# Attention and a Mish layer on one core: where a unit's first attention output is made

## The chip, the cores and the metric

The kernel runs on one core of one Trainium2 chip. The metric is the device time of one execution in microseconds, the median of several runs. Engines are called as the profile calls them: PE (matrix products), PEld (its weight loads), DVE (vector), ACT (activation), POOL and SP (which issues DMAs here).

## The reference

The inputs are q, k and v of 8 batches, 12 heads, 448 positions and 64 columns. For each head

```
scores = (q @ k.T) / 8
m      = max(scores, axis=-1)
e      = exp(scores - m)
attn   = e / (sum(e) + exp(-m) + 1e-9)
x      = attn @ v
```

The heads are put side by side into a matrix x of 3584 x 768. Then h = x @ w_in (768 x 2048), g = h * tanh(log(1 + exp(h))), which is the Mish function, and the result is g @ w_out (2048 x 768), in float32.

## The kernel before

**Pairs, units and stages.** Two heads make a pair; there are 48 pairs, six to a batch. From pair 6 on the kernel works in units of three pairs (`UNIT_PAIRS`), half a batch. The loop over `u` issues them: `p0 = 3 * u`, and unit `u` has two stages. In the first, 12 steps (`for n in range(steps)`) work on the scores of the unit's own pairs, on the attention outputs of the unit before, and on the last matrix product of earlier batches. In the second (`for f in range(FF_U)`) `mm1_mish` makes eight blocks of h and puts them through Mish; between them stand the denominators, the normalising of the unit's exponentials, their transposes by DMA, and the first scores of the next unit.

**A score group.** `scores(idx)` makes one of four groups of a pair. A group takes a score tile (`sc_tiles`, three tiles of two banks each). From pair 12 on (`DIAG_FROM`) the first three groups of a pair have two matmuls, one to each bank, and the fourth (`s == STEPS - 1`) has one, so its second bank is free. DVE then takes the maximum over the tile (L346). `exps(idx)` has ACT make the exponentials from the tile (L359), which gives the tile back. `scores_ahead` keeps three groups in the air: at step n of a unit group n + 3 is made, counted from 0 within the unit, while the exponentials are those of group n. Groups 0 to 2 of the next unit are made in the second stage.

**An attention output.** `av_pair(p)` (L459) multiplies the transposed exponentials `eT` of a pair by `v`: 8 matmuls in four pairs of 64 columns (L476). It goes into the bank that is given to it, or takes one with `mo_take`. The copy of the result to `xT` by DVE (a cast, L489) is put on the list `late`, and is issued at the next `flush_late()`, which stands at the start of every step behind the exponentials (L688), and wherever a part of the output product begins. `av_with` holds which output goes with which pair: `scores` makes it in front of the pair's fourth group, in the free second bank of that group's tile. So the three outputs of the unit before are made at steps 0, 4 and 8, each ahead of groups 3, 7 and 11.

**The output product.** `mm2_part(g, i, q0, nq)` makes a part of 128 rows and 192 or 384 columns (`nq` 1 or 2) in one bank: 16 matmuls (L565), issued two at a time as chunks. There are two such banks, `mo_tiles`, in the queue `mo_free`, which the second stage uses too. A part takes its bank with its first chunk. When its last chunk is issued, its copy to `o_sb` by DVE (L548) goes on `late`, and with that copy the bank goes back to the end of `mo_free`. An engine works through what is issued to it in order, so the place of that copy in DVE's row is where the list is flushed.

**The order of the chunks.** `plan` gives the parts of a unit. For odd `u` from 5 on their widths are 1, 2, 2, 2, for even `u` from 6 on 2, 2, 2, 1; the sum over the chunks is 56 in both. `weight` says how much is to be done by which step: 5.2 at step 0, 1.0 at each of steps 1 to 8, 0.4 at steps 9 to 11, of 14.4. That makes 20, 24, 28, 32 by the end of steps 0 to 3 in even units. A part of width 2 counts 16. So there the first part ends at step 0, the second at step 3, and the third begins at step 4. In odd units the parts end at 8, 24 and 40, the second at step 1, and the third begins at step 2. Within a step the order is: exponentials, flush, chunks, scores (with the output ahead of them).

**Other buffers that an output touches.** `eT` has three buffers, written by DMA transposes that SP issues in the second stage; `v_bf` has eight, written by POOL at step 0 of a unit; `xT` has two, one for each batch in work, and `mm1_mish` reads it.

Of the kernel before, what the change touches and what calls it, by code (L numbers as in the profile page):

```python
# [15 lines left out]
UNIT_PAIRS = 3  # L16
# [3 lines left out]
def kernel(  # L20
# [90 lines left out]
    av_with, av_read, rb = {}, {}, {}  # L111
# [6 lines left out]
    def mo_take():  # L118

        if not mo_free:  # L120
            flush_late()
        return mo_free.popleft()
# [104 lines left out]
    def apart(later, *earlier):  # L227

        for e in earlier:
            tc.declare_no_dep(later.ins, e.ins, reason="they read different PSUM banks")  # L230
# [63 lines left out]
    def free_half(p):  # L294

        return sc_tiles[(p * STEPS + STEPS - 1) % len(sc_tiles)][:, 1, :]

    def scores_ahead(limit):

        while rg["next"] < limit and rg["used"] < len(sc_tiles):  # L300
            rg["used"] += 1
            scores(rg["next"])
            rg["next"] += 1

    def scores(idx):

        p, s = divmod(idx, STEPS)
        if s == 0:
            if p < HP or p % UNIT_PAIRS == 0:
                for nm in ("negm", "sums", "expm", "den", "rden"):  # L310
                    stats[nm] = st_pool.tile([128, UNIT_PAIRS, NTILE], FP32, tag=nm, name=nm)
            at = 0 if p < HP else p % UNIT_PAIRS
            att[p] = {nm: t[:, at, :] for nm, t in stats.items()}
            att[p].update(en=en_bufs[p % N_EN], whole=dict(stats))
        st = att[p]
        qT, kT = qkT[p]
        kA, kB = kT[0:64, :], kT[64:128, :]
        sc = sc_tiles[idx % len(sc_tiles)]
        if s == STEPS - 1 and p in av_with:
            av_pair(av_with.pop(p), bank=sc[:, 1, :], beside=idx)  # L320
        if p >= DIAG_FROM:
            cols = tuple(range(2 * s, min(2 * s + 2, NTILE)))
            negm = st["negm"][:, cols[0] : cols[-1] + 1]
            for bk, i in enumerate(cols):
                nc.tensor.matmul(  # L325
                    sc[:, bk, 0:S], lhsT=qT[:, i].rearrange("d h r -> d (h r)"), rhs=kT,
                    start=True, stop=True,
                )
        elif s < 3:
            qa, qb = 128 * s, 64 + 128 * s  # L330
            nc.tensor.matmul(
                sc[:, 0, 0:S], lhsT=qT[0:64, qa : qa + 128], rhs=kA, start=True, stop=True
            )
            nc.tensor.matmul(
                sc[:, 1, 0:S], lhsT=qT[64:128, qb : qb + 128], rhs=kB, start=True, stop=True
            )
            cols, negm = (s, 4 + s), st["negm"][:, s : s + 5 : 4]
        else:
            nc.tensor.matmul(
                sc[0:64, 0, 0:S], lhsT=qT[0:64, 384:S], rhs=kA, start=True, stop=True  # L340
            )
            nc.tensor.matmul(
                sc[64:128, 0, 0:S], lhsT=qT[64:128, 0:64], rhs=kB, start=True, stop=True
            )
            cols, negm = (3,), st["negm"][:, 3:4]
        half_max[p] = nc.vector.tensor_reduce(  # L346
            out=negm, in_=sc[:, 0 : len(cols), 0:S], axis=AX.X, op=ALU.max, negate=True
        )
        st["sc", s] = (sc, cols)
# [109 lines left out]
    def av_pair(p, bank=None, beside=None, half=None, hold=False):  # L459
        b, hp = p // HP, p % HP  # L460
        eT = att[p]["eT"]
        v_bf = casted[p]["v"]
        if b not in xT:
            xT[b] = xT_pool.tile([128, DM_T, S], BF16, tag="xT", name="xT")
        if half is not None:
            bank = free_half(half)
            mms = av_beside.setdefault(half * STEPS + STEPS - 1, [])
        av = mo_take() if bank is None else bank
        for j in range(NT):
            for h in range(2):  # L470
                if p >= DIAG_FROM:
                    by_h = eT[0:SP_, j, :].rearrange("c (i h r) -> c h i r", h=2, r=64)
                    e_h = by_h[:, h]
                else:
                    e_h = eT[0:SP_, j, h * S : (h + 1) * S]
                mm = nc.tensor.matmul(  # L476
                    av[h * 64 : (h + 1) * 64, 0:S],
                    lhsT=v_bf[:, h, j * D : (j + 1) * D],
                    rhs=e_h,
                    start=(j == 0), stop=(j == NT - 1),  # L480
                )
                if half is not None:
                    apart(mm, half_max[half])
                    mms.append(mm)

        def evac():
            to = xT[b][:, hp, :]
            if p >= LATE_DIV:
                read = nc.vector.tensor_copy(out=to, in_=av[:, 0:S])  # L489
            else:  # L490
                read = nc.vector.tensor_tensor(
                    out=to, in0=av[:, 0:S], in1=rb.pop(p), op=ALU.mult
                )
            if half in half_exp:
                apart(read, half_exp[half])
            elif beside is not None or half is not None:
                av_read[beside if half is None else half * STEPS + STEPS - 1] = read
            if bank is None:
                mo_free.append(av)

        if p in spread_copy:
            late.append(spread_copy.pop(p))
        (held if hold else late).append(evac)
        del att[p], casted[p], qkT[p]
# [73 lines left out]
    first_mm2 = 2 * UNITS_PER_B  # L578
# [89 lines left out]
    for u in range(UNITS_PER_B, N_UNITS + 2 * UNITS_PER_B):  # L668
# [4 lines left out]
        total, done, acc = sum(w for _, w in filler), 0, 0.0  # L673
        p0 = u * UNIT_PAIRS
        if attn and u >= first_mm2:
            av_with.update({p0 + i: p0 + i - UNIT_PAIRS for i in range(UNIT_PAIRS)})
        nxt = p0 + UNIT_PAIRS
        end = min(nxt, N_PAIRS) * STEPS

        for n in range(steps):  # L680
            pi, s = divmod(n, STEPS)
            p, idx = p0 + pi, p0 * STEPS + n
# [22 lines left out]
            if n in LOAD_AT and u <= first_mm2 + 1:  # L705
                at = p0 + LOAD_AT.index(n)
# [41 lines left out]
            if u - UNITS_PER_B < len(W_AT):  # L748
                at = (u - UNITS_PER_B, n)
# [6 lines left out]
        for f in range(FF_U):  # L756
# [19 lines left out]
            if f in (3, FF_U - 1) and p0 >= LATE_DIV:  # L776
                p = todo[1 + f // (FF_U - 1)]
# [33 lines left out]
```

## Time and profile before

| what | value |
|---|---|
| median of 3 runs | 474.99 us |
| lowest and highest | 473.56 and 478.71 us |
| the profiled execution | 473.76 us |
| its span, first to last instruction | 472.0 us |
| mean granted clock of PE | 0.989 |
| PE busy | 449.1 us (95%) |
| DVE busy | 365.2 us (77%) |
| ACT busy | 332.4 us (70%) |
| matmuls of attention outputs (L476) into score banks | 336 recorded, 39.8 us |
| matmuls of the output product (L565) | 1024, 166.7 us |

How to read the views: a row of a timeline has the start in us from the span's start, the length in us, the engine, the line of the kernel, the operation, what it writes and reads with sizes, and the number of like instructions that were put together in the row. In brackets stands how long the engine was idle ahead of it, and what ended that. Rows of one engine can overlap a little, since instructions are pipelined. In the chain of waits a row has a start, a length and what the time went to.

### The profile page before, as it was taken

How to read it: one execution, taken by the hardware profiler on the slowest of the kernel's cores; microseconds unless marked ns; L12 is line 12 of the kernel's file. 1: busy time of each engine (PE TensorE's matmuls, PEld its weight loads, DVE VectorE, ACT ScalarE, POOL GpSimd, SP SyncE). 2: the span in 40 equal slices, each digit the busy share in tenths (PEclk: the TensorE clock that was granted, in tenths of full speed). 3: DMA queues.
4: the chain of work that ended last, by engine and by line, in shares of the span. 5: the costliest groups of instructions: out<-in, count | busy, mean ns of one | idle time of the engine just before them, and what ended most of it. 6: DMA issues, size and time to landing. Idle time of an engine off the chain costs nothing.

```text
span 472.0 us, 8866 instructions
## 1 busy us (share of the span) xinstructions
PE 449.1 (95%) x3051; PEld 246.8 (52%) x3051; DVE 365.2 (77%) x715; ACT 332.4 (70%) x877; POOL 103.0 (22%) x186
## 2 busy tenths in 40 slices
PE   6888999999998999999999999999999999999996
PEld 3344555545554555555555555555555555556563
DVE  5988848669897999999999999999899989421021
ACT  5999878888784869788796868687877869211300
POOL 4623555115023040311313040404040100000000
PEclk8889999999999999999999999999999999999999
DMA  8999999999899999999999999999999594921122
GB/s 228 239 205 230 235 219 212 176 255 202 199 272 244 233 251 223 264 238 227 272 251 241 228 252 209 292 201 254 235 291 226 159 214 121 231 71 33 35 65 69
DMA packets 232492, 97.93 MB, mean 207 GB/s; under 512 B 189312, under 2 KB 228992, under 8 KB 232448
## 3 DMA queue, kind: packets, MB, share of 16 engines
q1 hardware_dynamic: 224928, 91.06, 84.0%
q0 software_dynamic: 7488, 6.29, 9.1%
q8 instruction: 24, 0.39, 0.3%
q14 instruction: 20, 0.16, 0.2%
q10 hardware_dynamic: 32, 0.02, 0.0%
HBM read 45.61 MB, written 11.01 MB: 120 GB/s over the span
## 4 chain that ended last, share of the span: by engine, by line
PE 46%; DVE 20%; ACT 8%; DMA 6%; SPq 3%; issue 2%; POOL 0%; DVEq 0%; POOLq 0%
PE mo L512 17%; PE mo L565 16%; DVE negm L346 8%; ACT en L359 7%; DVE en L428 7%; PE sc L325 4%; PE sc L476 4%; DMA v_f<-in_v_dram 3%; PE sc L512 2%; DVE qd L266 2%; SPq L196 2%; DMA out_dram<-o_sb 1%; SPq L134 1%; DMA k_f<-in_k_dram 1%; DVE o_sb L548 1%
## 5 line engine op out<-in xcount | busy, mean ns | idle before, releaser
L359 ACT ACTIVATE en<-sc,negm 128x448 bf16<-128x448 f32 x336 | 208.7, 639 | 24.4 <-DVE negm L346 22.6
L346 DVE TENSOR_REDUCE negm<-sc 128x2 f32<-128x896 f32 x192 | 181.7, 969 | 27.0 <-PE sc L325 16.8
L565 PE MATMUL mo<-w_out_sb,gT 128*128 128x384 bf16 (+1 forms) x1024 | 166.7, 306 | 0.4 <-DVE rb L416 0.4
L512 PE MATMUL mo<-xT,w_in_sb 128*128 128x448 bf16 x672 | 138.6, 352 | 0.3 <-DVE xT L489 0.3
L565 PEld LDWEIGHTS <-gT 128*128 128x128 bf16 x1024 | 96.3, 98 | 56.0 <-issue 1.9
L518 ACT ACTIVATE gT<-mo 128x448 bf16<-128x448 f32 x112 | 59.3, 543 | 82.7 <-PE mo L512 82.5
L512 PEld LDWEIGHTS <-w_in_sb 128*128 128x128 bf16 x768 | 74.2, 98 | 68.8 <-issue 3.2
L428 DVE TENSOR_SCALAR en<-en,rden 128x448 bf16<-128x448 bf16 x252 | 83.4, 403 | 0.9
L325 PE MATMUL sc<-kT_all,qd 128*128 128x448 bf16 x252 | 71.6, 354 | 2.4 <-DVE qd L266 2.4
L185 POOL CAST v_bf<-v_f 112x512 bf16<-112x512 f32 x48 | 30.0, 629 | 198.0 <-DMA v_f<-in_v_dram 160.7
L359 ACT ACTIVATION_READ_ACCUMULATOR en<-sc,negm 128x1 f32 x336 | 70.7, 210 | 0.0
L548 DVE COPY o_sb<-mo 128x384 f32<-128x384 f32 (+1 forms) x64 | 31.9, 498 | 48.3 <-PE mo L565 48.1
L476 PE MATMUL sc<-eT,v_bf 112*64 112x448 bf16 x336 | 39.8, 357 | 3.9 <-ACT en L359 3.3
L325 PEld LDWEIGHTS <-qd 128*128 128x128 bf16 x252 | 24.3, 97 | 31.7 <-issue 12.9
L185 POOL CAST k_cast<-k_f 112x512 bf16<-112x512 f32 x47 | 29.6, 631 | 32.8 <-DMA k_f<-in_k_dram 24.4
L185 POOL CAST q_cast<-q_f 112x512 bf16<-112x512 f32 x47 | 29.6, 629 | 21.4 <-PE sc L325 14.3
L476 PEld LDWEIGHTS <-v_bf 112*64 112x64 bf16 x384 | 20.4, 109 | 22.3 <-issue 14.9
L266 DVE TENSOR_SCALAR qd<-qT_all 64x448 bf16<-64x448 bf16 x60 | 22.6, 377 | 4.1 <-DMA qT_all<-q_cast 3.4
L512 PE MATMUL sc<-xT,w_in_sb 128*128 128x448 bf16 x96 | 20.8, 352 | 0.0
L489 DVE CAST xT<-sc 128x448 bf16<-128x448 f32 x33 | 20.3, 615 | 0.0
L518 ACT ACT_TABLE_LOAD x14 | 18.0, 1283 | 0.8
L359 ACT ACT_TABLE_LOAD x13 | 16.7, 1283 | 0.2
(62 smaller groups left out, 231.1 us busy)
## 6 DMA issues: line engine op xcount, KB each, us to landing
k_f<-in_k_dram SPq DMA_DIRECT2D x48, 224.0 KB, 5.2
q_f<-in_q_dram SPq DMA_DIRECT2D x48, 224.0 KB, 4.8
v_f<-in_v_dram SPq DMA_DIRECT2D x48, 224.0 KB, 4.9
w_in_sb<-in_moe_w_in_dram POOLq DMA_DIRECT2D x12, 256.0 KB, 9.4
w_out_sb<-in_moe_w_out_dram POOLq DMA_DIRECT2D x8, 384.0 KB, 10.5
out_dram<-o_sb SPq DMA_DIRECT2D x7, 336.0 KB, 3.4
out_dram<-o_sb SPq DMA_DIRECT2D x8, 288.0 KB, 4.8
out_dram<-o_sb SPq DMA_DIRECT2D x8, 240.0 KB, 3.9
```

Of the source, the lines that this page charges most:

```text
L185: nc.gpsimd.tensor_copy(out=to[nm], in_=src)
L266: q_reads.append(nc.vector.tensor_scalar(out=qd[rows, :, h, :], in0=q_ps[rows, 0:S].rearrange("d (i r) -> d i r", i=QB), scalar1=SCALE, sc ...
L325: nc.tensor.matmul(sc[:, bk, 0:S], lhsT=qT[:, i].rearrange("d h r -> d (h r)"), rhs=kT, start=True, stop=True,)
L346: half_max[p] = nc.vector.tensor_reduce(out=negm, in_=sc[:, 0 : len(cols), 0:S], axis=AX.X, op=ALU.max, negate=True)
L359: e = nc.scalar.activation(out=st["en"][:, :, c, 0:SP_], in_=sc[:, bk, 0:S].rearrange("q (j c) -> q j c", j=NT), func=AF.Exp, bias=st["neg ...
L428: nc.vector.tensor_scalar(out=en[:, :, i, 0:SP_], in0=en[:, :, i, 0:SP_], scalar1=st["rden"][:, i : i + 1], scalar2=None, op0=ALU.mult,)
L476: mm = nc.tensor.matmul(av[h * 64 : (h + 1) * 64, 0:S], lhsT=v_bf[:, h, j * D : (j + 1) * D], rhs=e_h, start=(j == 0), stop=(j == NT - 1),)
L489: read = nc.vector.tensor_copy(out=to, in_=av[:, 0:S])
L512: nc.tensor.matmul(h_ps[:, 0:S], lhsT=w_in_sb[:, dm, ff * 128 : (ff + 1) * 128], rhs=xT[b][:, dm, :], start=(dm == 0), stop=(dm == DM_T - 1),)
L518: nc.scalar.activation(out=gT[:, ff, b % 2 * S : b % 2 * S + S], in_=h_ps[:, 0:S], func=AF.Mish)
L548: nc.vector.tensor_copy(out=o_sb[:, cols.start : cols.start + n_dve], in_=st["o"][:, 0:n_dve])
L565: nc.tensor.matmul(st["o"][:, 0:n_cols], lhsT=gT[:, ff, i * 128 : (i + 1) * 128], rhs=w_out_sb[:, ff, cols], start=(ff == 0), stop=(ff == ...
```

## The change

From unit 5 on (pair 15) the first output of the unit before is no longer made at step 0 with the first pair's fourth group, but at step 4, right in front of the second output. It gets no score bank: `av_pair(other)` without a bank takes one of the two `mo` banks, and its cast gives that bank back. The second output, in the score bank, follows it. The third stays at step 8. Unit 4 keeps the order of before; the units after the last pair, whose outputs always took `mo` banks, are not touched.

```
@@ in scores(idx)
         if s == STEPS - 1 and p in av_with:
-            av_pair(av_with.pop(p), bank=sc[:, 1, :], beside=idx)
+            *in_mo, in_sc = av_with.pop(p)
+            for other in in_mo:
+                av_pair(other)
+            av_pair(in_sc, bank=sc[:, 1, :], beside=idx)
@@ in the loop over u
         if attn and u >= first_mm2:
-            av_with.update({p0 + i: p0 + i - UNIT_PAIRS for i in range(UNIT_PAIRS)})
+            done_at = (0, 1, 2) if u == first_mm2 else (1, 1, 2)
+            for i, at in enumerate(done_at):
+                av_with.setdefault(p0 + at, []).append(p0 + i - UNIT_PAIRS)
```

## The prediction

> **What bounds the kernel now.** I read the page first, then the waits, then the timelines of PE, DVE and ACT of two neighbouring units, then the chain.
>
> ```profile
> PE 449.1 (95%) x3051; PEld 246.8 (52%) x3051; DVE 365.2 (77%) x715; ACT 332.4 (70%) x877; POOL 103.0 (22%) x186
> ```
>
> This is the page's line of busy times: PE is nearly full. In the view of waits the attention outputs that go into a score bank (PE sc L476) wait for exponentials (ACT en L359) 7 times, 3.3 us in all, 2.4 us of it in the units that the change touches. That is all the marked wait of theirs that the change could take from PE.
>
> I call the loop's units by their number u and the twelve score groups of a unit 0 to 11. Group 3 is made at step 0, group 7 at step 4, group 11 at step 8; these are the three whose second bank is free. The windows view, cut at the starts of the denominators (den), has units 7 and 8 as follows (length, then busy time and instructions of PE, PEld, DVE, ACT and POOL, granted clock, DMA share and rate):
>
> ```profile
> 168.22:193.81 25.59, 25.59 (x160) 13.86 (x158) 24.32 (x48) 20.40 (x54) 5.40 (x9) 1.00 1.05 233
> 193.81:219.12 25.31, 25.02 (x157) 13.87 (x156) 24.02 (x48) 20.16 (x53) 5.46 (x9) 1.00 1.12 227
> ```
>
> In odd units (7 to 15) the length is 25.57 to 25.59 us and PE is busy in all of it. In even ones (8 to 14) it is 25.31, 26.18, 25.75 and 25.58 us, with 25.01 to 25.18 us of PE. So PE bounds the odd units, and something else the even ones. The timeline of PE in u = 8 and, below it, that of DVE:
>
> ```profile
> 205.86 0.95 PE L476 MATMUL sc<-eT,v_bf 112*64 112x448 bf16 x8
> 206.74 0.36 PE L325 MATMUL sc<-kT_all,qd 128*128 128x448 bf16 x1
> ...
> 209.65 0.54 PE L325 MATMUL sc<-kT_all,qd 128*128 128x448 bf16 x2
> 210.03 0.81 PE L565 MATMUL mo<-w_out_sb,gT 128*128 128x384 bf16 x4
> 211.03 0.95 PE L476 MATMUL sc<-eT,v_bf 112*64 112x448 bf16 x8 [0.19 <-ACT en L359]
> 211.91 0.36 PE L325 MATMUL sc<-kT_all,qd 128*128 128x448 bf16 x1
> ```
>
> ```profile
> 207.46 0.61 DVE L346 TENSOR_REDUCE negm<-sc 128x1 f32<-128x448 f32 x1
> 207.99 0.61 DVE L489 CAST xT<-sc 128x448 bf16<-128x448 f32 x1
> 208.52 3.08 DVE L346 TENSOR_REDUCE negm<-sc 128x2 f32<-128x896 f32 x3
> 211.51 0.55 DVE L548 COPY o_sb<-mo 128x384 f32<-128x384 f32 x1
> 212.38 0.62 DVE L346 TENSOR_REDUCE negm<-sc 128x1 f32<-128x448 f32 x1 [0.32 <-PE sc L325]
> 212.92 0.61 DVE L489 CAST xT<-sc 128x448 bf16<-128x448 f32 x1
> 213.45 3.11 DVE L346 TENSOR_REDUCE negm<-sc 128x2 f32<-128x896 f32 x3
> ```
>
> DVE runs without a pause from the denominator to 212.06, and it is behind: group 6's scores were issued at 209.65, but its maximum is the third of the row at 208.52. Then the second output waits for ACT. The row to remember is the copy at 211.51. It empties the bank of the unit's second output-product part, whose last matmuls were done at 209.65; the copy stands in DVE's queue behind the maximum of group 6.
>
> The same place in an odd unit (u = 7), DVE and PE:
>
> ```profile
> 183.98 0.55 DVE L548 COPY o_sb<-mo 128x384 f32<-128x384 f32 x1
> 184.44 2.08 DVE L346 TENSOR_REDUCE negm<-sc 128x2 f32<-128x896 f32 x2
> 186.84 0.62 DVE L346 TENSOR_REDUCE negm<-sc 128x1 f32<-128x448 f32 x1 [0.31 <-PE sc L325]
> ```
>
> ```profile
> 184.71 0.81 PE L565 MATMUL mo<-w_out_sb,gT 128*128 128x384 bf16 x4
> 185.49 0.95 PE L476 MATMUL sc<-eT,v_bf 112*64 112x448 bf16 x8
> 186.37 0.36 PE L325 MATMUL sc<-kT_all,qd 128*128 128x448 bf16 x1
> ```
>
> Here the copy comes two maxima earlier, because odd units begin with a half-width part and end their second part at step 1.
>
> Last, the chain of waits at u = 16, where outputs go into the mo banks already:
>
> ```profile
> 409.37 0.57 DVE o_sb L548
> 409.94 0.04 issue
> 409.98 0.95 PE mo L476 x8
> ```
>
> An output product in a mo bank starts 0.04 us after the copy that frees the bank.
>
> **The change part by part.** Nothing is added or removed in number: per unit 8 matmuls, 8 weight loads and one cast move by four steps, in the 11 units u = 5 to 15 (pairs 15 to 47). The step issues no DMA and nothing on POOL or SP. What its inputs hold back there has room: the first eT buffer is written again by SP's transposes only after the denominator (219.12 in u = 8), some 7 us behind the new place, and v_bf has 8 buffers for at most 6 live pairs. Both cost nothing. The mark that keeps exponential and cast apart goes with group 3; it orders nothing else.
>
> (a) Step 0. PE is quicker by the output, 0.88 us (205.86 to 206.74), and by the change of shape in front of it, 0.09 us (20 matmuls of 0.163 us from 202.52 end at 205.78): 0.97 us. DVE loses one cast from its row, 0.53 us (207.99 to 208.52), so the maxima of groups 4 to 6 and what follows them come 0.53 us earlier where DVE is behind.
>
> (b) Step 4, the second bank. At step 4 one mo bank is held by the part in progress; the other is the one that the second part left. The output cannot start before that copy. Even units: the copy moves to 211.51 - 0.53 = 210.98, ends at 211.53, and with the 0.04 us of the chain the first output starts at 211.57. PE is there at 210.68 - 0.97 = 209.71 (210.03 and four matmuls of 0.163), so it waits 1.9 us, and all that is behind in its queue waits too: the second output, group 7's scores, the next parts. Odd units: the copy ends at 183.98 + 0.55 - 0.53 = 184.00 and PE comes at 185.36 - 0.97 + 0.09 = 184.48. No wait.
>
> (c) Two outputs in a row. The first costs four pairs of 0.19 us (12 matmuls of 448 columns take 2.27 us in the chain), 0.76 us, the second 0.88 us as before: 1.64 us to group 7's scores. Even: 211.57 + 1.64 = 213.21, against 211.91, +1.30 us. Odd: 184.48 + 1.64 = 186.12, against 186.37, -0.25 us.
>
> The gap of 0.09 us in front of an output, and 0.12 us behind (0.88 - 0.76), are the rows for a change of tile shape. The Trainium skill (TensorEngine Tiling, Key Properties) says that a change of tiling mode drains the array, and the trace agrees with about 0.2 us for a change there and back. Another of its pages (TensorE: Matmul & The Clock Gate, Part 2, on LDWEIGHTS) has the next weights load while the present matmul runs, by which joining two outputs would save nothing and the odd units would lose 0.2 us more each, 1.2 us in all; the rows decide for the first.
>
> (d) DVE at step 5. The maximum of group 7 waits for PE today (0.32 and 0.31 us), so it moves with the scores. Behind it stand now two casts, not one: +0.53 us before the maximum of group 8. Even: 1.30 + 0.53 = +1.83 us. Odd: -0.25 + 0.53 = +0.28 us.
>
> (e) Does it reach the end of the unit? ACT waits for group 8's maximum in both (0.51 us in u = 8, 0.28 in u = 7), and then runs its seven exponentials of groups 8 to 11 with hardly a pause up to expm, from which den starts. The third output waits for the exponentials of group 8 (they end at 190.37 in u = 7, it starts at 190.42), so PE loses what it had gained and takes the same shift. The first Mish of the next stage ends at 195.63 and PE takes up its bank at 195.71: no slack. So both shifts reach den and the next unit whole, as far as these rows go.
>
> (f) A cover. In odd units the fourth part starts at step 6 in the bank of the moved output. Its cast ends at 186.84 - 0.25 + 0.53 + 0.61 = 187.73, PE wants it at 187.60 - 0.25 = 187.35: 0.42 us of wait. It is hidden, since PE would reach the third output at 190.30 - 0.25 + 0.42 = 190.47 and must wait there until 190.70. Without that cover it would cost 6 x 0.42 = 2.5 us.
>
> Sum: 5 even units (6, 8, 10, 12, 14) x 1.83 = 9.15 and 6 odd ones x 0.28 = 1.68, together +10.8 us. The profiled execution took 473.76 us, so its like would take 484.6 us. It lies 1.23 us under the median of the runs shown, 474.99, from which the sum gives 485.8. I take the middle, 485.2 us.
>
> The unseen item is the price of an output that waits for a bank in the middle of a unit. From below: it is the lost PE time alone (first rival). From above: the shift whole, plus the spread of the even units. I take the whole shift, since den of u = 8 and all rows from group 8 on hang on ACT, which has no spare there.
>
> **The rivals.** First, smaller loss: the second cast and the odd units' 0.28 us are taken up by idle time that the two units do not show. Then remain 5 x 1.30 - 6 x 0.25 = +5.0 us, 478.8 on the profiled run and 479.4 on my scale. For it: DVE idles 1.3 us before group 3 in u = 5, 13 and 15. Against: that idle time lies ahead of the loss.
>
> Second, faster: the bank is free in time. This is decided by one point, that the copy of the second part ends before PE comes, 209.7 in u = 8. Then the output fills the time in which PE waits for ACT at step 4 (0.43, 0.19, 0.71, 0.63, 0.44 us in the even units, 2.4 us), 0.1 us at step 8 of these five (0.5 us), and 11 changes of shape of 0.21 us go (2.3 us): -5.2 us, 468.6, or 469.2 us. Against: in all five even units the copy stands behind the three maxima in DVE's row, 1.9 us too late.
>
> Third, greater loss: the cover of (f) is gone (2.5 us), and the even units, which are bound by DVE and vary from 25.31 to 26.18 us today, all meet the bad end (5 x 0.87 = 4.4 us): 485.2 + 6.9 = 492.1 us.
>
> Fourth, no change: PE takes up all by its 5% idle. Against: odd units have no idle PE time, and the even ones have at most 1.0 us (26.18 - 25.18), less than 1.83.
>
> **How the numbers follow.** My sum: 0.74. Smaller loss 0.12, greater loss 0.08, faster 0.04, no change 0.02. The sum's own range is 482 to 488 (0.2 us of error in each of 11 units, and the 1.2 us between profiled run and median). The range 480 to 489.5 takes in most of the way to the smaller loss and a third of that to the greater one. A measurement of this kernel can tell about 1% from no change, 4.7 us. Faster by more than that: 0.04. Slower: my sum, the greater loss and a part of the smaller one, 0.87. Within: 0.09.
>
> **What would show it.** In the profile after: in even units a wait of PE at L476, on a mo tile, of about 1.9 us (before it stood for ACT on sc), with a copy o_sb just done; in odd units none there. DVE: two casts xT in a row at step 5, idle 2 us before group 7's maximum in even units. ACT idle before group 8 up by 1.8 or 0.3 us over today on its clock of the unit. From den to den some 27.1 us in u = 8 and 25.9 in odd units. The prediction is wrong if the output in the even units starts without a wait, or if den to den does not grow by what group 8 loses.

## The result and the profile after

The changed kernel takes 489.28 us (median of 6 runs, 487.90 to 492.27). The kernel before took 474.27 us in the median of 6 runs beside it. The ratio is 1.031, with a 95% interval of 1.026 to 1.036: slower by 3.1%, 15.0 us. I had forecast 485.2 us in a range of 480.0 to 489.5, slower by more than 1% with a chance of 0.87. The direction and the place are right; the size is 4 us short, and lies only 0.2 us inside the range. That it lies inside is luck: the upper bound took in a third of the greater loss, whose first cause, the lost cover of step (f), is not what happened. The profiled execution took 489.5 us, its span is 487.7 us.

The page's line of busy times after; the work is the same, PE's share fell by two points:

```profile
PE 452.5 (93%) x3051; PEld 248.8 (51%) x3051; DVE 367.1 (75%) x715; ACT 332.9 (68%) x877; POOL 103.0 (21%) x186
```

Lines of the kernel after are three further down than those of before from the edit on: the outputs are L479, the output product L568, the copy L551, the maxima L349, the casts L492, the normalising L431. Units 7 and 8 in the windows view, cut at the denominators (length, busy time and instructions of PE, PEld, DVE, ACT, POOL, clock, DMA):

```profile
170.30:197.76 27.46, 26.03 (x160) 13.93 (x158) 24.74 (x49) 20.47 (x54) 5.34 (x9) 1.00 0.95 208
197.76:225.22 27.46, 25.24 (x157) 13.99 (x156) 24.24 (x49) 20.32 (x53) 5.60 (x9) 1.00 1.01 234
```

Unit 7 grew by 1.87 us, unit 8 by 2.15. Over the whole kernel, from den to den after less before, in us:

| unit | 5 | 6 | 7 | 8 | 9 | 10 | 11 | 12 | 13 | 14 | 15 |
|---|---|---|---|---|---|---|---|---|---|---|---|
| grew by | 0.68 | 1.61 | 1.87 | 2.15 | 0.81 | 1.50 | 1.41 | 2.26 | 0.84 | 2.08 | 0.73 |

The sum is 15.9 us; the head of the kernel is 0.2 us shorter after, its tail the same (73.05 us from the last den before, 73.04 after). The five even units took 9.6 us, where I had 9.15. The six odd ones took 6.3 us, where I had 1.7.

The waits of PE after (who waited for whom: us in all, times, longest):

```profile
PE mo L479 <- DVE o_sb L551: 6.1, 5, 1.5
PE sc L328 <- DVE qd L266: 5.1, 6, 1.6
PE sc L479 <- ACT en L362: 3.5, 6, 0.6
...
PE mo L568 <- DVE xT L492: 1.7, 6, 0.3
```

The first row is the forecast: five even units, each with a wait for the copy that frees the bank. The last is the six odd units' wait for the moved output's own bank. The second row I had not priced; it stood at 2.4 us before, in two places.

**An even unit.** PE and below it DVE in u = 8 after:

```profile
213.15 0.54 PE L328 MATMUL sc<-kT_all,qd 128*128 128x448 bf16 x2
213.53 0.81 PE L568 MATMUL mo<-w_out_sb,gT 128*128 128x384 bf16 x4
215.77 0.95 PE L479 MATMUL mo<-eT,v_bf 112*64 112x448 bf16 x8 [1.44 <-DVE o_sb L551]
216.53 0.95 PE L479 MATMUL sc<-eT,v_bf 112*64 112x448 bf16 x8
217.41 0.36 PE L328 MATMUL sc<-kT_all,qd 128*128 128x448 bf16 x1
...
221.99 0.95 PE L479 MATMUL sc<-eT,v_bf 112*64 112x448 bf16 x8 [0.64 <-ACT en L362]
```

```profile
211.65 3.61 DVE L349 TENSOR_REDUCE negm<-sc 128x1 f32<-128x448 f32 x4
215.17 0.55 DVE L551 COPY o_sb<-mo 128x384 f32<-128x384 f32 x1
217.88 0.63 DVE L349 TENSOR_REDUCE negm<-sc 128x1 f32<-128x448 f32 x1 [2.16 <-PE sc L328]
218.42 0.61 DVE L492 CAST xT<-mo 128x448 bf16<-128x448 f32 x1
218.95 0.61 DVE L492 CAST xT<-sc 128x448 bf16<-128x448 f32 x1
219.48 3.08 DVE L349 TENSOR_REDUCE negm<-sc 128x2 f32<-128x896 f32 x3
```

The reader sees the whole of the main step. The copy ends at 215.72 and the output starts at 215.77. DVE, which made PE wait, then waits itself 2.16 us for the scores that stand behind the two outputs, does two casts in a row, and only then takes group 8's maximum. The third output waits 0.64 us for ACT. Start to start, PE stood for 1.60 us behind the row at 213.53 (its four matmuls of 0.163 us are over at 214.18); the bracket has 1.44, since a matmul's end is modelled later than the next one may start.

**An odd unit.** PE in u = 9 after; the gaps are found from start to start, at 0.163 us for a matmul of the output product and 0.19 for one of 448 columns:

```profile
237.51 0.35 PE L328 MATMUL sc<-kT_all,qd 128*128 128x448 bf16 x1
237.70 0.81 PE L568 MATMUL mo<-w_out_sb,gT 128*128 128x384 bf16 x4
238.60 0.54 PE L328 MATMUL sc<-kT_all,qd 128*128 128x448 bf16 x2
239.12 0.81 PE L568 MATMUL mo<-w_out_sb,gT 128*128 128x384 bf16 x4
239.83 0.54 PE L328 MATMUL sc<-kT_all,qd 128*128 128x448 bf16 x2
...
241.98 0.95 PE L479 MATMUL mo<-eT,v_bf 112*64 112x448 bf16 x8
242.76 0.92 PE L479 MATMUL sc<-eT,v_bf 112*64 112x448 bf16 x8
243.62 0.36 PE L328 MATMUL sc<-kT_all,qd 128*128 128x448 bf16 x1
243.82 0.81 PE L568 MATMUL mo<-w_out_sb,gT 128*128 128x384 bf16 x4
244.47 0.54 PE L328 MATMUL sc<-kT_all,qd 128*128 128x448 bf16 x2
245.30 0.81 PE L568 MATMUL mo<-w_out_sb,gT 128*128 128x384 bf16 x4 [0.29 <-DVE xT L492]
...
247.35 0.81 PE L568 MATMUL mo<-w_out_sb,gT 128*128 128x384 bf16 x4
248.20 0.95 PE L479 MATMUL sc<-eT,v_bf 112*64 112x448 bf16 x8
```

Three rows of ACT and DVE in the same unit, to which PE's starts belong:

```profile
238.34 0.21 ACT L362 ACTIVATION_READ_ACCUMULATOR en<-sc,negm 128x1 f32 x1
238.71 0.35 DVE L551 COPY o_sb<-mo 128x192 f32<-128x192 f32 x1
247.95 0.20 ACT L362 ACTIVATION_READ_ACCUMULATOR en<-sc,negm 128x1 f32 x1
```

No wait at the moved output, as forecast. But the lead that I carried to it is nearly half gone: PE stands for 0.25 us at 238.60 (group 4 needs the tile of group 1, whose last exponential ACT ends at 238.55), 0.14 at 239.12 (the first part's bank, whose copy ends at 239.06) and 0.06 at 239.83, 0.45 us in all. In unit 15, which nothing else disturbs, it is 0.25 and 0.20 us, ahead of the scores of groups 4 and 5, and both end 0.05 us behind ACT's last exponential of the group whose tile they need (groups 1 and 2). At 245.30 it stands for 0.45 us for the cast of the moved output, since the fourth part takes that bank.

### The profile page after: what moved, and what is told of

Same layout as the page of the kernel before. It is cut to its first block, busy times and chain, and to the rows that moved or that the text cites. A ratio compares the mean times of both kernels' runs of the same rounds, so it can differ in the third digit from the quotient of the medians.

```text
span 487.7 us, 8854 instructions
## 1 busy us (share of the span) xinstructions
PE 452.5 (93%) x3051; PEld 248.8 (51%) x3051; DVE 367.1 (75%) x715; ACT 332.9 (68%) x877; POOL 103.0 (21%) x186
## 4 chain that ended last, share of the span: by engine, by line
PE 43%; DVE 20%; ACT 12%; DMA 5%; issue 3%; SPq 2%; POOL 0%; DVEq 0%; ACTq 0%; POOLq 0%
PE mo L515 17%; PE mo L568 12%; ACT en L362 9%; DVE negm L349 8%; DVE en L431 6%; PE sc L328 5%; PE sc L479 3%; ACT L362 2%; PE mo L479 2%; PE sc L515 2%; DMA k_f<-in_k_dram 2%; DMA v_f<-in_v_dram 2%; DVE xT L492 2%; DVE qd L266 2%; SPq L196 1%
## 5 line engine op out<-in xcount | busy, mean ns | idle before, releaser
L349 DVE TENSOR_REDUCE negm<-sc 128x2 f32<-128x896 f32 x192 | 181.7, 969 | 41.9 <-PE sc L328 31.5
L568 PE MATMUL mo<-w_out_sb,gT 128*128 128x384 bf16 (+1 forms) x1024 | 166.6, 306 | 2.1 <-DVE xT L492 1.7
L568 PEld LDWEIGHTS <-gT 128*128 128x128 bf16 x1024 | 96.2, 98 | 59.7 <-issue 5.4
L431 DVE TENSOR_SCALAR en<-en,rden 128x448 bf16<-128x448 bf16 x252 | 84.0, 404 | 0.9
L551 DVE COPY o_sb<-mo 128x384 f32<-128x384 f32 (+1 forms) x64 | 31.9, 498 | 48.3 <-PE mo L568 48.1
L479 PEld LDWEIGHTS <-v_bf 112*64 112x64 bf16 x384 | 22.0, 109 | 26.5 <-issue 18.5
L479 PE MATMUL sc<-eT,v_bf 112*64 112x448 bf16 x248 | 29.2, 355 | 4.3 <-ACT en L362 3.5
L479 PE MATMUL mo<-eT,v_bf 112*64 112x448 bf16 x136 | 16.1, 357 | 6.2 <-DVE o_sb L551 6.1
```

The source lines that it names most:

```text
L349: half_max[p] = nc.vector.tensor_reduce(out=negm, in_=sc[:, 0 : len(cols), 0:S], axis=AX.X, op=ALU.max, negate=True)
L431: nc.vector.tensor_scalar(out=en[:, :, i, 0:SP_], in0=en[:, :, i, 0:SP_], scalar1=st["rden"][:, i : i + 1], scalar2=None, op0=ALU.mult,)
L479: mm = nc.tensor.matmul(av[h * 64 : (h + 1) * 64, 0:S], lhsT=v_bf[:, h, j * D : (j + 1) * D], rhs=e_h, start=(j == 0), stop=(j == NT - 1),)
L551: nc.vector.tensor_copy(out=o_sb[:, cols.start : cols.start + n_dve], in_=st["o"][:, 0:n_dve])
L568: nc.tensor.matmul(st["o"][:, 0:n_cols], lhsT=gT[:, ff, i * 128 : (i + 1) * 128], rhs=w_out_sb[:, ff, cols], start=(ff == 0), stop=(ff == ...
```

## The experiments

Times are medians; ratios are to runs of the kernel before beside them, with 95% intervals. The per-unit figures are of one profiled execution each.

**1 and 2: the change in odd units alone, and in even units alone.**

```
-            done_at = (0, 1, 2) if u == first_mm2 else (1, 1, 2)
+            done_at = (1, 1, 2) if u > first_mm2 and u % 2 == 1 else (0, 1, 2)   # run 1
+            done_at = (1, 1, 2) if u > first_mm2 and u % 2 == 0 else (0, 1, 2)   # run 2
```

> The new order in the six odd units (5, 7, 9, 11, 13, 15) alone; even units keep the order of before. In the profile after, den to den grew in the odd units by 0.68, 1.87, 0.81, 1.41, 0.84 and 0.73 us. Theory: an odd unit has a loss of its own, about 0.73 us, because PE's lead from step 0 is lost again at waits in steps 1 and 2 (0.45 us) and the second cast costs 0.28 us; the surplus in units 7 and 11 comes from where POOL's casts fall on DVE's normalising. Then 474.3 + 6 x 0.73 = 478.7 us, up to 480.6 us if the surplus comes too. Rival, the predicted 0.28 us for an odd unit: 476.0 us.

Measured: 479.29 us, ratio 1.010 (1.002 to 1.018). Odd units grew by 0.69, 1.52, 0.78, 2.02, 0.74 and 0.74 us, even ones by 0.2 us together. So an odd unit has a loss of its own of 0.7 us, not 0.28, and units 7 and 11 have a surplus without any help of the even ones.

> The new order in the five even units (6 to 14) alone. Theory: the wait for the bank of the second part and the second cast cost what den to den grew by in the even units after, 1.61, 2.15, 1.50, 2.26 and 2.08 us: 474.3 + 9.6 = 483.9 us, with five waits of PE for o_sb at the moved output of 1 to 1.9 us each, and odd units at 25.6 us from den to den. Rival, that the losses of the two kinds of unit come from each other (POOL and DMA drifting against DVE): the two halves then do not add up to 489.3 - 474.3 = 15.0 us, and this one lies under 481 us.

Measured: 485.94 us, ratio 1.024 (1.015 to 1.032). Five waits of PE for the copy at the moved output, 7.1 us in all, and the even units grew by 7.9 us. But odd units 7, 9, 11 and 13, which have their old order here, grew by 1.22, 0.53, 0.92 and 0.81 us, where I had expected none; in each of them PE waits once in the second stage, 0.35 to 1.06 us, ahead of the next unit's first scores (three times for qd, once for ACT). The spans are 5.5 us longer in run 1 and 10.8 in run 2, together 16.3, against 15.7 us of both. Over units 5 to 15 alone the halves make 18.1 us against 15.9. So they add only to within about 2 us, and a term that travels between the units is left over.

**3: the second output's cast one step later.**

```
-        (held if hold else late).append(evac)
+        by_step = beside is not None and p >= DIAG_FROM and beside % 12 != 11
+        (held if hold else slow if by_step else late).append(evac)
```

> The changed kernel, but the cast of the second output is issued one step later, behind the maximum of group 8, so that one cast, not two, stands ahead of that maximum. Theory: the path to the unit's end runs over that maximum and ACT, so each of the 11 units gains one cast, 0.53 us: 489.3 - 5.8 = 483.5 us. Rival, that the lost time is PE's wait alone and the second cast is hidden: no change, 489.3 us. Second rival, that the cast only moves the delay to group 9 and so on: a gain under 2 us.

Measured: 487.81 us, ratio 1.025 (1.018 to 1.032), an interval that overlaps that of the change, so the time does not tell the two rivals apart. The profile speaks for the second: group 8's maximum comes earlier, but the cast now stands ahead of group 9's, and group 10's scores wait 0.10 to 0.14 us for it in even units. In unit 15, which has no other disturbance, den to den is 26.15 us against 26.30. Counted from the unit's first scores, group 9's maximum starts no sooner (17.45 us in both), and the third output 0.10 us sooner (18.39 against 18.49). It does not wait for ACT there, but PE still waits 0.45 us at the fourth part on the way.

**4: the half-width part first in the even units (6 to 14).**

```
-            plan[u0] = rest + whole(g, 0) + [(g, 1, 0, 1)]
+            plan[u0] = [(g, 1, 0, 1)] + rest + whole(g, 0)
...
-        plan[u0 + 2] = whole(g, 3) + [(g, 4, 0, 2), (g, 4, 2, 1)]
+        plan[u0 + 2] = [(g, 4, 2, 1)] + whole(g, 3) + [(g, 4, 0, 2)]
```

> The changed kernel, but even units from 8 on begin with their half-width part as odd units do, so that the second part ends at step 1 and its copy is long done when the moved output wants its bank (unit 6 too). Theory: no wait of PE for o_sb at the moved output any more, and an even unit loses what an odd one loses, 0.7 us in place of 1.9: 5 x 1.2 = 6 us less, 483.3 us. Rival, that the bank is not what sets the even units: 489 us, the same end with the wait in another place (for exponentials or the score tile).

Measured: 485.07 us, ratio 1.020 (1.013 to 1.026). From the waits of PE in that run:

```profile
PE mo L568 <- DVE xT L492: 3.1, 11, 0.3
```

The row for the copy at the moved output is gone, and all 11 units have the odd units' wait for the moved output's cast. Even units lost 4.4 us in all over before, not 9.6. So the place of the copy sets about 5 of the 9.6 us, as the theory has it. Run 6 below is the base for this run, the kernel before with the same edit: its ratio is 1.006, so with the odd units' order in all units the change costs about 1.3%, not 3.1%.

**5: two idle matmuls at step 0.**

```
+        if s == STEPS - 1 and p >= 15 and p % UNIT_PAIRS == 0:
+            keep_busy(2, bank=sc[:, 1, :])
```

> The changed kernel with two matmuls of 448 columns on constants put in at step 0 of units 5 to 15, where the first output was, in the free second bank of group 3's tile; their result is not used. They take 0.38 us of PE. Theory: PE cannot use the lead that the missing output gives it; it is lost at the score tile of group 4 (ACT), at the bank of the first part (copy by DVE) and, in even units, at the moved output. So the two are free: 489.3 us, within 1 us, and the waits of PE in steps 1 and 2 shrink by as much. Rival, PE is the bound and each matmul costs its time: 11 x 0.38 = 4.2 us, 493.5 us.

Measured: 488.24 us, ratio 1.031 (1.028 to 1.035); the change itself has 1.031. They are free. In unit 15:

```profile
399.77 0.54 PE L286 MATMUL sc<-busy 128*128 128x448 bf16 x2
400.15 0.35 PE L330 MATMUL sc<-kT_all,qd 128*128 128x448 bf16 x1
400.34 0.81 PE L570 MATMUL mo<-w_out_sb,gT 128*128 128x384 bf16 x4
400.99 0.54 PE L330 MATMUL sc<-kT_all,qd 128*128 128x448 bf16 x2
401.37 0.81 PE L570 MATMUL mo<-w_out_sb,gT 128*128 128x384 bf16 x4
402.10 0.54 PE L330 MATMUL sc<-kT_all,qd 128*128 128x448 bf16 x2
```

The waits ahead of groups 4 and 5 have shrunk to 0 and 0.08 us, and the unit is as long as without the two, 26.31 us against 26.30. So of the 0.97 us that the output gave back at step 0, at least these 0.38 us were of no use to anything behind it.

**6, 7 and 8: the edits of 4 and 3 in the kernel before, alone and together.** In run 7 the later cast is that of the first output too.

> The kernel before, with the half-width part first in even units. It is the base for the same edit of the changed kernel. If the edit by itself shortens DVE's row in the even units (0.27 us less of copy ahead of group 3), they come from 25.3 to 26.2 us to the 25.6 us of the odd ones: 1 to 2 us less, 472.5 us. If even units are bound by something else: 474.3 us.

> The kernel before, with the casts of the first and second output of units 5 to 15 issued one step later, behind the maximum of groups 4 and 8. Theory: even units are bound by DVE and ACT, with casts of 0.53 us in the path ahead of both maxima, so they fall from 25.3 to 26.2 us to PE's own 25.1 us, and odd units, full of PE work, stay at 25.6: 2 to 4 us less, 471 us. Rival: PE bounds both, no change, 474.3 us.

> The kernel before with both edits, the half-width part first and the casts one step later. If the two gains are of the same idle time of the even units, it is as fast as the better of the two, 471 us; if they add, 469.5 us; if neither path matters, 474.3 us.

Measured: 477.26 us (ratio 1.006, 1.002 to 1.010), 482.52 us (1.017, 1.011 to 1.022) and 485.72 us (1.027, 1.022 to 1.031). All three expectations of a gain fell. In run 6 even units 8 to 14 changed by 0.01, -0.12, -0.34 and 0.14 us, and unit 6 and the odd units 7, 11 and 13 grew, with waits for qd. In runs 7 and 8 the later cast holds a score tile: group 6's scores wait for it (PE waits 1.2 us in all for such casts in run 8), and unit 15, which has no other disturbance, goes from 25.57 to 26.06 us in run 8. A cast that is put behind one maximum keeps the next group's scores waiting for its tile; the order of before was the better one.

**9 and 10: POOL's casts left out.** Scores use the casts of pairs 15 to 17 again, outputs the v of pair 17, in both kernels.

```
+    SILENT_FROM, v_kept = 18, [None]
...
-                to[nm] = bf_pool.tile([SP_, 2, NT * D], BF16, tag="v_bf", name="v_bf", bufs=8)
+                if p < SILENT_FROM:
+                    v_kept[0] = bf_pool.tile([SP_, 2, NT * D], BF16, tag="v_bf", name="v_bf", bufs=8)
+                to[nm] = v_kept[0]
+            if p >= SILENT_FROM:
+                continue
```

> The kernel before without POOL's casts of q, k and v from pair 18 on: the score matmuls use the casts of pairs 15 to 17 again and the outputs the v of pair 17; loads, transposes and all other work stay. It is the base for the next run. Theory: a normalising row of DVE takes 0.33 us alone and 0.68 us beside a cast of POOL, so without the casts DVE's row in the second stage shrinks by 1.5 to 3 us per unit; the wait of PE for qd (2.4 us in all) goes, even units come down to PE's 25.1 us, odd ones stay at 25.6: some 4 us less, 470 us. Rival: DVE is as slow without the casts: 474.5 us.

> The changed kernel with the same casts left out. Theory: of the 15 us of the change, the part that comes from where the casts fall on DVE's normalising goes (PE's wait for qd, 5.1 us after against 2.4 before, so 2.65 us); waits of PE for qd in units 7, 10, 11, 12 and 14 are gone, odd units 7 and 11 lose 0.7 us like the others. The even units' wait for the bank shrinks only if DVE's row in steps 0 to 4 is no longer behind; it runs from the denominator without a pause, so with 1.5 to 3 us less of normalising it is no longer behind, the copy comes as soon as its part is done, and the wait at the moved output falls under 0.5 us. Then the two kernels without casts differ by 3 to 6 us. Rival, that the even units' loss does not hang on DVE's being behind: they differ by 12 us.

Measured: 470.47 us (ratio 0.992, 0.989 to 0.996) for the kernel before without casts, and 486.21 us (1.026, 1.021 to 1.032) for the changed one. Units 10 and 11 of both in the windows view, before first:

```profile
246.05:271.12 25.07, 24.96 (x157) 13.76 (x156) 22.36 (x49) 20.07 (x53) 0.00 (x0) 1.00 1.03 260
271.12:296.69 25.57, 25.57 (x161) 13.85 (x159) 22.30 (x49) 20.43 (x54) 0.00 (x0) 1.00 1.04 229
```

```profile
254.03:281.00 26.97, 25.11 (x157) 14.12 (x156) 22.53 (x48) 20.16 (x53) 0.00 (x0) 1.00 0.98 229
281.00:307.31 26.31, 25.85 (x161) 14.02 (x159) 22.40 (x48) 20.50 (x54) 0.00 (x0) 1.00 0.97 223
```

Without the casts the units are regular. From 8 on all even units of before are 25.07 or 25.08 us and all odd ones 25.57 or 25.58; of the changed kernel 26.96 to 27.02 and 26.31 to 26.39. The bare price of the change is 1.89 us for an even unit and 0.74 for an odd one, and the waits for qd of units 7 to 14 are gone from both.

My expectation for the pair was wrong: the two kernels differ by 15.7 us, not by 3 to 6, and the rival's 12 us came nearer. I had held that the wait for the bank comes from DVE being behind, and falls under 0.5 us when it is not. DVE and PE in u = 10 of the changed kernel without casts:

```profile
267.74 3.35 DVE L355 TENSOR_REDUCE negm<-sc 128x2 f32<-128x896 f32 x3 [0.75 <-PE sc L334]
271.01 0.55 DVE L557 COPY o_sb<-mo 128x384 f32<-128x384 f32 x1
```

```profile
269.73 0.81 PE L574 MATMUL mo<-w_out_sb,gT 128*128 128x384 bf16 x4
271.61 0.95 PE L485 MATMUL mo<-eT,v_bf 112*64 112x448 bf16 x8 [1.07 <-DVE o_sb L557]
```

DVE waits 0.75 us for scores ahead of the three maxima, so it is in time here, and PE still waits 1.07 us. The first of the three maxima starts 0.65 us behind the start of group 4's scores (267.09), and three maxima and a copy are 3.8 us of DVE: 4.5 us from there to the bank. PE's work from the same point is three steps of 1.03 us (a group's scores 0.38, four matmuls 0.65) and 0.2 us of waits, 3.3 us. The wait is built into the order.

**11: the copy one maximum earlier.** In even units the list is flushed at the end of step 3's chunks, so that the second part's copy stands ahead of group 6's maximum.

```
+            if attn and u > first_mm2 and u % 2 == 0 and n == 3:
+                flush_late()
```

> The changed kernel, with the copy of the second part in even units issued at the end of step 3's chunks, one maximum (1.0 us) earlier in DVE's row, ahead of that of group 6. Theory: the moved output's wait for the bank falls by 1.0 us, from 1.1 to 1.5 us to 0.1 to 0.5 us, and the even units by as much: 5 us less, 484 us. Rival, that the wait moves to group 6's late maximum, which is 0.47 us later: 2 us less or nothing, 487 to 489 us.

Measured: 486.95 us, ratio 1.030 (1.024 to 1.036). By its profile the wait for the bank fell from 6.1 to 1.1 us and the even units lost 5.25 us, not 9.6; the span is 3.3 us shorter. In units 12 and 14 PE still waits 0.60 and 0.32 us there from start to start, where it waited 1.23 in both with the change alone. The interval of the runs overlaps that of the change, so the gain in time is not shown; that the wait follows the copy is.

## Why the prediction was right, and where it was short

Step (b), the bank: right. In all five even units the moved output waits for the second part's copy and starts 0.05 us behind its end. The wait is 1.23 to 1.68 us from start to start, not 1.9, since PE comes later than I had it (step (a)). Runs 4 and 11 move the copy and the wait goes with it. The rival by which the bank is free in time is refuted. That DVE's being behind makes this wait, as I read the rows, is not so (run 10): where DVE is behind it adds up to 0.45 us to a floor of 1.06.

Step (c), two outputs in a row: right. They take 1.64 us (215.77 to 217.41), as worked out; a change of shape is saved, and no gap stands between the two (215.77 and 0.76 us are 216.53). The Trainium skill (TensorEngine Tiling, Key Properties) says that a change of tiling mode drains the array; the trace agrees with a gap at each change and none between like shapes.

Steps (d) and (e): right. The second cast is there in full, the shift goes on to the denominator, and no idle time took it up, so the first rival is refuted. In u = 8, counted from the denominator ahead of the unit, group 7's maximum starts 1.56 us later than in the kernel before, group 8's 2.09, which is 0.53 more, and the unit ends 2.15 later. For an odd unit take DVE in u = 15, the kernel before first; the denominators ahead of the unit start at 373.36 and 388.36:

```profile
391.96 0.62 DVE L346 TENSOR_REDUCE negm<-sc 128x1 f32<-128x448 f32 x1 [0.31 <-PE sc L325]
392.50 0.61 DVE L489 CAST xT<-sc 128x448 bf16<-128x448 f32 x1
393.03 1.08 DVE L346 TENSOR_REDUCE negm<-sc 128x2 f32<-128x896 f32 x1
```

```profile
407.15 0.62 DVE L349 TENSOR_REDUCE negm<-sc 128x1 f32<-128x448 f32 x1 [1.29 <-PE sc L328]
407.69 0.61 DVE L492 CAST xT<-mo 128x448 bf16<-128x448 f32 x1
408.23 0.61 DVE L492 CAST xT<-sc 128x448 bf16<-128x448 f32 x1
408.76 1.08 DVE L349 TENSOR_REDUCE negm<-sc 128x2 f32<-128x896 f32 x1
```

Counted from there, group 7's maximum starts at 18.6 us in the kernel before and at 18.8 in the changed one, group 8's at 19.67 and 20.40, and the unit takes 25.57 and 26.30 us: later by 0.20, 0.73 and 0.73 us. That run 3 got so little for moving the cast does not speak against this: it stands ahead of group 9's maximum there, and that starts no sooner. The sum for an even unit, 1.83 us, came out at 1.89 without casts of POOL and at 1.92 in the mean with them.

Step (a) is the one that failed: "PE is quicker by the output ... and by the change of shape in front of it: 0.97 us". I carried all of it to step 4 in odd units. 0.45 us is lost on the way: in the undisturbed unit 15 at the score tiles of groups 1 and 2, which ACT gives back, in u = 9 at the first of them and at the bank of the first part, which DVE gives back. Run 5 shows it: 0.38 us of matmuls put back there cost nothing. So group 7's scores come 0.20 us later, not 0.25 earlier, and with the second cast an odd unit loses 0.20 + 0.53 = 0.73 us; 0.74 were measured without casts. My +0.28 was short by the lost lead alone, 6 x 0.46 = 2.8 us.

Step (f), the cover: right, though with less to spare. The wait at the fourth part is there, 0.45 us from start to start against 0.42, and it is still hidden. In u = 9 PE is done with the row at 247.35 at 248.00, and 0.09 us for the change of shape make 248.09; the third output starts at 248.20, 0.05 us behind the last exponential of group 8, as in the kernel before (190.37 and 190.42 in u = 7). So ACT still sets that point, by 0.11 us, and the third rival's 2.5 us for a lost cover did not come; a loss of about that size came from the lead.

The rest I had not in the sum. At the lengths without casts the change costs 5 x 1.89 + 6 x 0.74 = 13.9 us. In units 7 to 15 the profiles with casts have 13.65 us where that makes 11.3 (4 x 1.89 + 5 x 0.74); the 2.4 us more go with where POOL's casts fall. This stands on one profiled execution of each kernel: the medians of the runs do not show it, since the kernels differ by 15.0 us with the casts and by 15.7 without. A first block of normalising in the two kernels, unit 7 after and unit 10 of before without casts, on DVE:

```profile
171.25 3.93 DVE L431 TENSOR_SCALAR en<-en,rden 128x448 bf16<-128x448 bf16 x7
```

```profile
246.59 1.81 DVE L434 TENSOR_SCALAR en<-en,rden 128x448 bf16<-128x448 bf16 x7
```

POOL casts without a pause from 170.24 to 175.65 there. Seven rows then take twice as long, qd comes late, and PE stands for 1.04 us at the next unit's first scores. Over the lengths without casts, units 7 to 14 of before are 2.55 us longer, all in even units; odd ones, full of PE work, lost none. After they are 4.9 us longer, in units of both kinds. The casts begin at the denominator there (170.24 against 170.30), and 1.4 and 1.6 us behind it in units 8 and 9; before, 0.7, 1.8 and 3.5 us behind it in units 7 to 9. In these three units after, the profile has the first cast wait for the load of v. Why it comes sooner there, no run here tells apart; it is left open. The third rival, the greater loss, had a spread of the even units in it, 4.4 us, at a chance of 0.08 together with (f).

## What to carry to other kernels

Moving a step to "a free bank" is priced by the copy that frees the bank, and by what stands ahead of that copy in the copying engine's row; look for it by step, since two kinds of unit with the same parts in another order had 1.1 to 1.5 us and none. A lead is only worth what the next instructions can use of it: before counting it as won, list what they wait for, here the score tiles that ACT gives back. And read gaps on PE from start to start, for the brackets leave out waits shorter than the modelled tail.

## What the runs showed of the hardware

A normalising instruction of DVE (tensor_scalar, bf16, 128 x 448) took 0.33 us alone and 0.68 us beside a cast of POOL, and with the casts left out none of them was over 0.34 us in units 7 to 15. The Trainium skill (SBUF — State Buffer, Who interferes with whom) says that a tensor_scalar of DVE can take a pair of ports that it shares with GpSimd (POOL here), and that whichever is first then fully blocks the other. The doubling agrees with that; the ports themselves no trace here shows. The kernel before gains 0.8% (0.4 to 1.2) from leaving the casts out, so their place, not only their length, is worth a look in this kernel.
